# Folded attention weight in blocks of whole heads, moved to 128-row chunks by transfers within SBUF

## The chip, the core and the metric

One of the eight cores of a Trainium2 chip runs the kernel. A core has five engines, each with its own stream of instructions: TensorE (PE, matrix multiplication; PEld is its weight load), VectorE (DVE), ScalarE (ACT), GpSimd (POOL) and SyncE (SP), which here only issues transfers (DMA). The engines wait for one another through semaphores. The working memory SBUF has 128 partitions, and matmuls write to PSUM, eight banks of 512 float32 columns on 128 partitions. The metric is the device time of one execution in microseconds; the median of the runs is compared.

## The reference

The input x has 2048 tokens of 640 features in bfloat16. Both branches read the same layer-normalised x:

```python
xn = layernorm(x)
q, k, v = split(xn @ wqkv)                       # 32 heads of 20 features
pq, pk = phi(q), phi(k)                          # phi(t) = (t + 1 if t > 0 else exp(t)) + 1e-6
kv  = einsum("bhsd,bhse->bhde", pk, v)           # 20 x 20 for each head
z   = einsum("bhsd->bhd", pk)
num = einsum("bhqd,bhde->bhqe", pq, kv)
den = einsum("bhqd,bhd->bhq", pq, z)[..., None] + 1e-6
s   = merge_heads(num / den) @ wo                # 640 x 640
g   = silu(relu(xn @ w1) @ w2)                   # 640 -> 1728 -> 640
out = x + s * g
```

## The kernel before

All intermediate data stay in SBUF. Tokens are handled in 16 tiles of 128 or 4 chunks of 512, features in 5 chunks of 128 and the 1728 hidden features in 13 chunks of 128 and a rest of 64. The order of the work on each engine is the order in which the program text emits it; a small scheduler class only works out which semaphores an instruction has to wait for.

The program goes through these stages:

1. **Normalisation and projections** (to 111 us). x is loaded, normalised and transposed. Blocks of keys (`K_mm`, L473), queries (`Q_block`, L541) and hidden features (`H_mm`, L556) are interleaved on TensorE. ScalarE and VectorE form `pk`, `pqT` (transposed queries after phi) and `hT`. GpSimd adds up z. At the end stand `z_col` (L633; VectorE multiplies its result by a mask, L637), the last hidden blocks, the rest of 64 hidden features (`H_halves`, L578) and the denominators (`den`, L646), whose reciprocal VectorE takes (L654).
2. **Transfers behind it.** SP issues the loads of w2 (L756, L760), four stores that write the reciprocal denominators, each repeated for the 20 features of its head, to a scratch in HBM (L763), two loads of wo in blocks of 120 rows (L767, L769), and five loads that bring the scratch back as `rep` (L772). SP works its list in order.
3. **Gram blocks** (`G_block`, L787, 111 to 133 us). `GT = xn^T pk`, five blocks of 32 matmuls. ScalarE copies each block to SBUF (L792). Values are never formed: kv is `wv^T GT`, of which only the 20 x 20 blocks on the diagonal are kept.
4. **Folded weight** (133 to 153 us). `kv_block` (L799) multiplies, for six heads (120 rows) at a time, `wv^T GT`; VectorE masks the diagonal blocks into `kvp` (L802), a 640-column row of blocks whose other columns GpSimd has zeroed (L907). `W_block` (L813) then forms the product of kv and wo, `wf`, in five chunks of 128 rows. A chunk of 128 rows cuts through blocks of 120, so each chunk adds up two blocks, in two halves of 320 columns: 20 matmuls. The last block has only 40 rows. ScalarE copies each chunk to SBUF (L818). Between these stand pieces of the down projection `U_main` (L831), 13 matmuls of 320 columns for each tile and half, `U_halves` (L847) for the rest of 64, and the gate's silu (L862, L865). VectorE multiplies `pqT` by `rep` (`divide`, L778).
5. **Output tiles** (153 us to the end). `s_tile` (L877) is `pqT x wf`, 10 matmuls a tile; VectorE multiplies by the gate (L899) and adds x (L884), which has been loaded a second time (L909, issued after the gram blocks); SP stores the tile (L887). Each output tile stands between pieces of the down projection of the next pair of tiles.

The buffers share memory: `wo_sb` lies where x was loaded, `GT` and `wf` lie where the query and key weights were, `kvp` where `pk` was, `rep` and the gates where the transposed normalised x was, and the second x where the normalised x was. PSUM banks go round by hand: the gram blocks use banks 0 to 3, `kv_block` 0 to 3, the first pair of down-projection tiles 4 to 7.

The two loops that the change replaces are these:

```python
    U_main(0, 0)
    for c in range(VC):
        kv_block(c, c % 4)
    for m in range(C):
        divide(m)
    U_main(0, 1, (0,))
    W_block(0, 0)
    W_block(1, 2)
```

Of the kernel before, what the change touches and what calls it, by code (L numbers as in the profile page):

```python
# [211 lines left out]
def bass_recurrent_scan__linear_attn_block__dense_activation_relu__prompt_kernel(  # L212
# [26 lines left out]
    VR = HC * DH  # L239
    VC = -(-D // VR)  # L240

    def vrows(c):
        return min(VR, D - VR * c)

    def cs_of_m(m):
        return [c for c in range(VC) if VR * c < P * (m + 1) and VR * c + vrows(c) > P * m]

    x2 = A_x[0]
    out2 = out[0]
# [13 lines left out]
    NOUT = 4  # L263
    reg3 = nc.alloc_sbuf_tensor("reg3", [P, T * D], bf)
    pk = reg3[:, :].rearrange("p (t n) -> p t n", t=T)
    kvp = reg3[:, 0:VC * D].rearrange("p (c n) -> p c n", c=VC)
    outb = reg3[:, VC * D:(VC + NOUT) * D].rearrange("p (a n) -> p a n", a=NOUT)
    tmpo = reg3[:, (VC + NOUT) * D:(VC + 2 * NOUT) * D].rearrange("p (a n) -> p a n", a=NOUT)
    pqT = nc.alloc_sbuf_tensor("pqT", [P, C, S], bf)
# [12 lines left out]
    xq0 = wqk[:, :, D:D + 512]  # L282
    GT = reg6[:, 0:C * D].rearrange("p (c n) -> p c n", c=C)
    wf = reg6[:, C * D:2 * C * D].rearrange("p (c n) -> p c n", c=C)
    wv_sb = nc.alloc_sbuf_tensor("wv_sb", [P, C, D], bf)

    reg7 = nc.alloc_sbuf_tensor("reg7", [P, XR * D], bf)
# [35 lines left out]
    def dma(E, fn, R=(), W=(), extra=()):  # L323
        i = nds[0]
        nds[0] += 1
        return sc.dma(E, fn, i, R=R, W=W, extra=extra)
# [77 lines left out]
    def xnk(t, cs=range(C)):  # L404
        return [("xn", t, c) for c in cs]
# [300 lines left out]
    for j in range(1, J):  # L706
        qs = [("q", j, f) for f in range(C)]
        hs = [("h", j, f) for f in range(NF)]
        if j == J - 1:
            qs += [("q", 0, f) for f in range(C)]  # L710
        blocks = []
        while qs or hs:
            if qs:
                blocks.append(qs.pop(0))
            for _ in range(2 if j + 1 < J else 1):
                if hs:
                    blocks.append(hs.pop(0))
        for n, (kind, jj, f) in enumerate(blocks):
            if kind == "q":
                Q_block(jj, f)  # L720
            else:
                lastX = H_block(jj, f)
            if j + 1 < J:
                t0 = 4 * (j + 1)
                if n in (0, 2, 4, 6):
                    LN_stats(t0 + n // 2)
                if n in (1, 3, 5, 7):
                    LN_norm(t0 + n // 2)
                    xnT_dma(t0 + n // 2)
                if n in (9, 12, 14, 17):  # L730
                    t = t0 + (9, 12, 14, 17).index(n)
                    K_mm(t, 0)
                    K_ev(t, 0)
                if n in (8, 10, 12, 14, 16):
                    z_add()
                if j == 1 and n == 16:
                    build_masks()
            else:
                if n == 0:
                    for t in range(4):  # L740
                        dma("SP", lambda eng, t=t: eng.dma_start_transpose(xq0[:, :, tok(t)], xn[:, t, :]),
                            R=xnk(t), W=[("xq0", t)], extra=[lastK[0]])
                if n % 2 == 0 and zpend:
                    z_add()
                    if not zpend:
                        z_split()
                if n == 18:
                    z_col()
                if n == 20:
                    H_halves()  # L750
                    den()
    assert not zpend

    for a in range(2):
# [7 lines left out]
    for i in range(J):  # L762
        dma("SP", lambda eng, i=i: eng.dma_start(  # L763
            rscr[:, schunk(i)].rearrange("(h d) s -> h d s", d=DH),
            rden[H * i:H * (i + 1), :].unsqueeze(1).to_broadcast([H, DH, 512])), R=[("rden",)], W=[("rscr", i)])
    nfull = (VC - 1) * VR
    dma("SP", lambda eng: eng.dma_start(wo_sb[0:VR, 0:VC - 1, :], A_wo[0:nfull, :].rearrange("(c p) n -> p c n", p=VR)),  # L767
        W=[("wo", 0)], extra=[last_norm[0]])
    dma("SP", lambda eng: eng.dma_start(wo_sb[0:D - nfull, VC - 1, :], A_wo[nfull:D, :]),  # L769
        W=[("wo", 1)], extra=[last_norm[0]])  # L770
    for c in range(C):
        dma("SP", lambda eng, c=c: eng.dma_start(rep[:, c, :], rscr[P * c:P * (c + 1), :]),  # L772
            R=[("rscr", i) for i in range(J)], W=[("rep", c)], extra=[lastX])
# [20 lines left out]
        return ag  # L794

    def kv_block(c, b):
        n0, nr = VR * c, vrows(c)
        w = P if n0 + P <= D else nr
        sc.group("PE", [(lambda eng, k=k: eng.matmul(ps[b][0:w, 0:nr], lhsT=wv_sb[:, k, n0:n0 + w],  # L799
                                                     rhs=GT[:, k, n0:n0 + nr], start=(k == 0), stop=(k == C - 1)))  # L800
                        for k in range(C)], R=[("wv",)] + [("GT", k) for k in range(C)], W=[("ps", b)])
        sc.op("DVE", lambda eng: eng.tensor_tensor(  # L802
            out=kvp[0:nr, c, n0:n0 + nr].rearrange("p (h e) -> p h e", e=DH),
            in0=ps[b][0:nr, 0:nr].rearrange("p (h e) -> p h e", e=DH),
            in1=m6[0:nr, 0:nr // DH].unsqueeze(2).to_broadcast([nr, nr // DH, DH]), op=ALU.mult),
            R=[("ps", b), ("m6",), ("kvz",)], W=[("kv", c)])

    def W_block(m, b):
        cs = cs_of_m(m)
        fns = []  # L810
        for a in range(2):
            for ci, c in enumerate(cs):
                fns.append(lambda eng, a=a, c=c, ci=ci: eng.matmul(  # L813
                    ps[b + a][:, 0:HN], lhsT=kvp[0:vrows(c), c, P * m:P * (m + 1)],
                    rhs=wo_sb[0:vrows(c), c, HN * a:HN * (a + 1)],
                    start=(ci == 0), stop=(ci == len(cs) - 1)))
        sc.group("PE", fns, R=[("wo", 0), ("wo", 1), ("kvz",)] + [("kv", c) for c in cs], W=[("ps", b), ("ps", b + 1)])
        sc.op("ACT", lambda eng: eng.activation(out=two(wf[:, m, :]), in_=ps2(b, HN),  # L818
                                                func=ACTF.Copy), R=[("ps", b), ("ps", b + 1)], W=[("wf", m)])


    pairs = [(4 * jj + q, 4 * jj + q + 4) for jj in (0, 2) for q in range(4)]
# [46 lines left out]
    def s_tile(p, u, b, last=False):  # L869
        t = pairs[p][u]  # L870
        os_ = so[0] % NOUT
        so[0] += 1
        i = t // 4

        parts = [(b, 0, HN), (b + 1, HN, 512), (bank(7, 0), 512, D)] if last else [(b, 0, HN), (b + 1, HN, D)]
        for pb, lo, hi in parts:
            sc.group("PE", [(lambda eng, c=c, pb=pb, lo=lo, hi=hi: eng.matmul(  # L877
                ps[pb][:, 0:hi - lo], lhsT=pqT[:, c, tok(t)], rhs=wf[:, c, lo:hi],
                start=(c == 0), stop=(c == C - 1))) for c in range(C)],
                R=[("pqT", i, c) for c in range(C)] + [("wf", c) for c in range(C)], W=[("ps", pb)])  # L880
        gk = [("g", t, 0), ("g", t, 1)]

        def add(E, lo, hi, keys):
            sc.op(E, lambda eng: eng.tensor_tensor(out=outb[:, os_, lo:hi], in0=tmpo[:, os_, lo:hi],  # L884
                                                   in1=xre[:, t, lo:hi], op=ALU.add),
                  R=[("tmpo", os_, k) for k in keys] + [("xre", t // 4)], W=[("outb", os_, k) for k in keys])
            dma("SP", lambda eng: eng.dma_start(out2[tok(t), lo:hi], outb[:, os_, lo:hi]),  # L887
                R=[("outb", os_, k) for k in keys])

        if last:  # L890
            for k, (pb, lo, hi) in enumerate(parts):
                sc.op("DVE", lambda eng, pb=pb, lo=lo, hi=hi: eng.tensor_tensor(  # L892
                    out=tmpo[:, os_, lo:hi], in0=ps[pb][:, 0:hi - lo], in1=g_sb[:, t, lo:hi], op=ALU.mult),
                    R=[("ps", pb)] + gk, W=[("tmpo", os_, k)])
                if k == 0:
                    add("POOL", lo, hi, (0,))
            add("DVE", HN, D, (1, 2))
        else:
            sc.op("DVE", lambda eng: eng.tensor_tensor(  # L899
                out=two(tmpo[:, os_, :]), in0=ps2(b, HN), in1=two(g_sb[:, t, :]), op=ALU.mult),  # L900
                R=[("ps", b), ("ps", b + 1)] + gk, W=[("tmpo", os_, k) for k in range(3)])
            add("DVE", 0, D, (0, 1, 2))

    lastG = None
    for k in range(C):
        lastG = G_block(k, (0, 2)[k % 2])
    sc.op("POOL", lambda eng: eng.memset(kvp, 0.0), W=[("kvz",)], extra=[lastG])  # L907
    for jx in range(4):
        dma("SP", lambda eng, jx=jx: eng.dma_start(  # L909
            xre[:, 4 * jx:4 * jx + 4, :], x2[512 * jx:512 * (jx + 1), :].rearrange("(t p) n -> p t n", p=P)),  # L910
            W=[("xre", jx)], extra=[lastG])

    lo, hi = range(7), range(7, NF)
    U_main(0, 0)
    for c in range(VC):
        kv_block(c, c % 4)
    for m in range(C):
        divide(m)
    U_main(0, 1, (0,))
    W_block(0, 0)  # L920
    W_block(1, 2)
    U_main(0, 1, (1,))
    U_halves((0, 1))
    U_silu(0, 0)
    U_silu(0, 1)
    U_main(1, 0)
    W_block(2, 4)
    W_block(3, 6)
    U_silu(1, 0)
    U_main(1, 1, (0,))  # L930
    W_block(4, 4)
    U_main(1, 1, (1,))
    U_silu(1, 1)
    s_tile(0, 0, 4)
    s_tile(0, 1, 6)
# [53 lines left out]
```

## Time and profile before

| what | value |
|---|---|
| median of 3 runs | 224.97 us (224.68 to 225.07) |
| the profiled execution's own time | 224.7 us |
| its span | 223.0 us |
| granted TensorE clock | 1.0 throughout |
| TensorE busy | 97% of the span |
| VectorE, ScalarE, GpSimd busy | 51%, 38%, 21% |
| gram blocks, folded weight stage, output stage | 111.4 to 133.2, 133.2 to 152.9, 152.9 to 223.0 us |

The span runs from the first to the last instruction that the profile shows; the execution's own time has 1.7 us around it. Times in the rows count from the start of the span. In the rows of the timeline the columns are start, length (from the first start to the last end of a merged run of instructions), engine, line, operation, the tile written and those read, the shape, the count, and in brackets the idle time before it with what ended it. A matmul's own length (299 ns for 320 columns) is its passage through the array; the next one starts long before it has ended, so that the distance of two starts is what a matmul costs. `120*128` stands for a weight tile of 120 rows and 128 columns. In rows by line, the three numbers behind the count are the shortest, median and longest length in ns. In rows of waits the columns are the total, the number of times and the longest wait in us. In the rows of transfer issues the last number is the median time from issue to landing in us, and in the row of a stretch of time the last three are the granted clock, the transfer engines' busy share and GB/s. In rows of the chain the columns are start, length, engine, tile, line and count.

### The profile page before, as it was taken

What the parts mean: (1) busy time and instruction counts of PE and PEld (TensorE: products, weight loads), DVE (VectorE), ACT (ScalarE), POOL (GpSimd) and SP (SyncE); (2) the same over time, 40 slices, a digit from 0 to 9 for tenths busy, and PEclk for the clock granted to TensorE, in tenths of its full rate; (3) what the DMA queues carried; (4) which work ended last, traced back from release to release, by engine and by line L of the source; (5) the groups of instructions that cost most, each with busy time, mean ns of one, the idle gap of its engine ahead of it and who ended that gap; (6) DMA issues with size and microseconds to landing.
All of it is one profiled execution on the core that took longest, in us unless ns stands there. A gap on an engine that the chain in (4) does not pass through costs nothing.

```text
span 223.0 us, 3534 instructions
## 1 busy us (share of the span) xinstructions
PE 216.9 (97%) x1471; PEld 133.9 (60%) x1482; DVE 114.4 (51%) x193; ACT 85.3 (38%) x137; POOL 47.0 (21%) x67
## 2 busy tenths in 40 slices
PE   7999999999999999999999999999999999999993
PEld 2865554455545554444477777666767776776672
DVE  2788836789686999986330004803322222314062
ACT  2467765567656565555321120632021102110300
POOL 4053101269123998600000004000000000000001
PEclk9999999999999999999999999999999999999999
DMA  6899580211012105000089999940110100000011
GB/s 205 232 379 231 118 249 21 59 39 23 0 29 59 32 1 118 0 0 3 0 257 361 240 223 374 369 154 0 59 59 3 60 29 32 29 29 32 29 54 64
DMA packets 27432, 23.73 MB, mean 106 GB/s; under 512 B 11673, under 2 KB 26777, under 8 KB 27417
## 3 DMA queue, kind: packets, MB, share of 16 engines
q1 hardware_dynamic: 26761, 23.03, 35.1%
q10 hardware_dynamic: 656, 0.49, 0.7%
q8 instruction: 11, 0.18, 0.3%
q14 instruction: 4, 0.03, 0.0%
HBM read 15.65 MB, written 5.24 MB: 94 GB/s over the span
## 4 chain that ended last, share of the span: by engine, by line
PE 95%; DVE 1%; DMA 1%; issue 0%; ACT 0%
PE psT L831 26%; PE psT L556 25%; PE psT L787 10%; PE psT L473 10%; PE psT L541 10%; PE psT L877 9%; PE psT L813 1%; DMA reg<-in_A_x_dram 1%; PE psT L847 1%; PE psT L578 1%; PE psT L799 1%; PE psT L646 1%; PE psT L451 0%; DVE reg L892 0%; DVE stats L393 0%
## 5 line engine op out<-in xcount | busy, mean ns | idle before, releaser
L556 PE MATMUL psT<-reg 128*128 128x512 bf16 (+1 forms) x295 | 59.8, 347 | 0.7 <-issue 0.2
L831 PE MATMUL psT<-reg,hT 128*128 128x320 bf16 x416 | 60.2, 299 | 0.0
L831 PEld LDWEIGHTS psT<-reg,hT 128*128 128x128 bf16 x416 | 40.2, 98 | 16.6 <-issue 1.1
L556 PEld LDWEIGHTS psT<-reg 128*128 128x128 bf16 x305 | 27.3, 98 | 27.0 <-issue 0.4
L899 DVE TENSOR_TENSOR reg<-psT,reg 128x640 bf16<-128x640 f32 x15 | 12.4, 824 | 53.1 <-PE psT L877 53.1
L563 ACT ACTIVATE hT<-psT 128x512 bf16<-128x512 f32 x52 | 30.9, 599 | 19.4 <-PE psT L556 19.4
L865 ACT ACTIVATE reg<-psT 128x640 bf16<-128x640 f32 (+1 forms) x13 | 8.4, 661 | 42.8 <-PE psT L831 23.3
L541 PE MATMUL psT<-reg 128*128 128x512 bf16 x99 | 24.6, 379 | 0.1
L473 PE MATMUL psT<-reg 128*128 128x320 bf16 x160 | 24.2, 299 | 0.0
L482 POOL TENSOR_TENSOR zacc<-zacc,reg 128x640 f32<-128x640 f32 x16 | 23.7, 1483 | 1.9 <-DVE reg L516 1.0
L877 PE MATMUL psT<-reg,pqT 128*128 128x320 bf16 (+2 forms) x165 | 24.0, 295 | 0.0
L787 PE MATMUL psT<-reg 128*128 128x320 bf16 x160 | 21.9, 299 | 0.0
L473 PEld LDWEIGHTS psT<-reg 128*128 128x128 bf16 x160 | 15.6, 98 | 8.2
L877 PEld LDWEIGHTS psT<-reg,pqT 128*128 128x128 bf16 x165 | 15.9, 98 | 6.0
L787 PEld LDWEIGHTS psT<-reg 128*128 128x128 bf16 x160 | 15.6, 98 | 6.2
L884 POOL TENSOR_TENSOR reg<-reg 128x320 bf16<-128x320 bf16 x1 | 0.8, 786 | 82.6 <-DVE reg L892 82.6
L551 DVE SCALAR_TENSOR_TENSOR pqT<-er 128x512 bf16<-128x512 bf16 x20 | 17.1, 854 | 0.7
L541 PEld LDWEIGHTS psT<-reg 128*128 128x128 bf16 x100 | 9.7, 98 | 11.6 <-DVE er L549 0.6
L393 DVE BATCH_NORM_STATS2 stats<-reg 128x6 f32<-128x320 bf16 x32 | 14.0, 479 | 3.4 <-DMA reg<-in_A_x_dram 3.4
L548 ACT ACTIVATE er<-psT 128x512 bf16<-128x512 f32 x20 | 12.0, 598 | 8.9 <-PE psT L541 8.1
L549 DVE TENSOR_SCALAR er<-psT 128x512 bf16<-128x512 f32 x20 | 13.6, 679 | 3.0 <-ACT er L548 3.0
L516 DVE TENSOR_TENSOR reg<-ek 128x640 bf16<-128x640 bf16 x16 | 13.5, 843 | 1.5 <-ACT ek L507 1.0
(67 smaller groups left out, 137.7 us busy)
## 6 DMA issues: line engine op xcount, KB each, us to landing
reg<-in_A_x_dram SPq DMA_DIRECT2D x16, 160.0 KB, 3.8
rscr<-rden SPq DMA_DIRECT2D x4, 640.0 KB, 10.8
reg<-rscr SPq DMA_DIRECT2D x5, 512.0 KB, 8.5
reg<-in_A_x_dram SPq DMA_DIRECT2D x4, 640.0 KB, 11.5
out_dram<-reg SPq DMA_DIRECT2D x15, 160.0 KB, 1.8
reg<-in_A_wqkv_dram SPq DMA_DIRECT2D x2, 800.0 KB, 6.7
reg<-in_B_w_dram SPq DMA_DIRECT2D x1, 1120.0 KB, 5.6
reg<-in_B_w_dram SPq DMA_DIRECT2D x1, 1040.0 KB, 7.7
```

The lines of the kernel that those rows point to most:

```text
L393: sc.op("DVE", lambda eng, a=a: eng.bn_stats(stats[:, t, a, :], xv[:, HN * a:HN * (a + 1)]), R=[("xin", t % XR)], W=[("stats", t, a)])
L473: fns.append(lambda eng, a=a, k=k: eng.matmul(ps[b + a][:, 0:HN], lhsT=xnT[:, k, tok(t)], rhs=wqk[:, k, D + HN * a:D + HN * (a + 1)], star ...
L482: sc.op("POOL", lambda eng: eng.tensor_tensor(out=zacc[:, :], in0=zacc[:, :], in1=pk[:, t, :], op=ALU.add), R=[("zacc",), ("pk", t)], W=[( ...
L516: sc.op("DVE", lambda eng: eng.tensor_tensor(out=pk[:, t, :], in0=e_, in1=r_, op=ALU.add), R=[("ek_e", es), ("ek_r", es)], W=[("pk", t)])
L541: sc.group("PE", [(lambda eng, k=k: eng.matmul(ps[b], lhsT=wqk[:, k, P * f:P * (f + 1)], rhs=rhs(k), start=(k == 0), stop=(k == C - 1))) f ...
L549: sc.op("DVE", lambda eng: eng.tensor_scalar(out=r_, in0=ps[b], scalar1=0.0, scalar2=1e-6, op0=ALU.max, op1=ALU.add), R=[("ps", b), ("er_e ...
L551: sc.op("DVE", lambda eng: eng.scalar_tensor_tensor(out=pqT[:, f, schunk(j)], in0=e_, scalar=1.0, in1=r_, op0=ALU.min, op1=ALU.add), R=[(" ...
L556: return sc.group("PE", [(lambda eng, k=k: eng.matmul(ps[b][:, lo:hi], lhsT=w1_sb[:, k, P * f:P * (f + 1)], rhs=xnT[:, k, 512 * j + lo:512 ...
L563: sc.op("ACT", lambda eng: eng.activation(out=hT[:, f, schunk(j)], in_=ps[b], func=ACTF.Relu), R=[("ps", b)], W=[("hT", j, f)])
L787: fns.append(lambda eng, t=t, a=a: eng.matmul(ps[b + a][:, 0:HN], lhsT=xn[:, t, P * k:P * (k + 1)], rhs=pk[:, t, HN * a:HN * (a + 1)], sta ...
L831: sc.group("PE", [(lambda eng, f=f, n=n: eng.matmul(ps[b + n][:, 0:HN], lhsT=hT[:, f, tok(t)], rhs=w2_sb[:, f, HN * n:HN * (n + 1)], start ...
L877: sc.group("PE", [(lambda eng, c=c, pb=pb, lo=lo, hi=hi: eng.matmul(ps[pb][:, 0:hi - lo], lhsT=pqT[:, c, tok(t)], rhs=wf[:, c, lo:hi], sta ...
```

## The change

The folded weight is now formed in the blocks of 120 rows themselves, each by two matmuls, since a block of six whole heads needs no other block. The sixth block starts at row 520 in place of 600, so that it too has 120 rows; of these only the last 40 are used. The zeros around the blocks, and the memset that writes them, go. ScalarE copies block 0 to its place in `wf`; the other five go to a staging buffer that lies where `GT` was, and SP moves their rows into the 128-row chunks of `wf` by transfers within SBUF: two each for blocks 1 to 4 (8 + 112, 16 + 104, 24 + 96, 32 + 88 rows) and one for block 5 (40 rows). The output tiles wait for all of these.

The weights that `kv_block` loads are now 120 columns wide in all six blocks; before, five of them were 128 wide with 120 used, and the last 40.

The order changes too. The six `kv_block`s stand behind 7 matmuls of the down projection, where they stood behind 26, and the folded blocks are spread over the first pair's down projection. The second load of x is issued behind the last move instead of right after the gram blocks. The loads of wo stand behind the four transposes of the first chunk (L741) on SP instead of between the stores and loads of the denominators. `den` stands ahead of `H_halves`.

```diff
+    V0 = [min(VR * c, D - VR) for c in range(VC)]
...
-    kvp = reg3[:, 0:VC * D].rearrange("p (c n) -> p c n", c=VC)
+    kvp = reg3[:, 0:VC * VR].rearrange("p (c n) -> p c n", c=VC)
...
+    wh = GT
...
                     for t in range(4):
                         dma("SP", lambda eng, t=t: eng.dma_start_transpose(xq0[:, :, tok(t)], xn[:, t, :]),
                             R=xnk(t), W=[("xq0", t)], extra=[lastK[0]])
+                    dma("SP", lambda eng: eng.dma_start(
+                        wo_sb[0:VR, 0:VC - 1, :], A_wo[0:VR * (VC - 1), :].rearrange("(c p) n -> p c n", p=VR)),
+                        W=[("wo", 0)], extra=[last_norm[0]])
+                    dma("SP", lambda eng: eng.dma_start(wo_sb[0:VR, VC - 1, :], A_wo[D - VR:D, :]),
+                        W=[("wo", 1)], extra=[last_norm[0]])
...
                 if n == 20:
+                    den()
                     H_halves()
-                    den()
...
-    nfull = (VC - 1) * VR
-    dma("SP", lambda eng: eng.dma_start(wo_sb[0:VR, 0:VC - 1, :], A_wo[0:nfull, :].rearrange("(c p) n -> p c n", p=VR)),
-        W=[("wo", 0)], extra=[last_norm[0]])
-    dma("SP", lambda eng: eng.dma_start(wo_sb[0:D - nfull, VC - 1, :], A_wo[nfull:D, :]),
-        W=[("wo", 1)], extra=[last_norm[0]])
...
     def kv_block(c, b):
-        n0, nr = VR * c, vrows(c)
-        w = P if n0 + P <= D else nr
-        sc.group("PE", [(lambda eng, k=k: eng.matmul(ps[b][0:w, 0:nr], lhsT=wv_sb[:, k, n0:n0 + w],
-                                                     rhs=GT[:, k, n0:n0 + nr], start=(k == 0), stop=(k == C - 1)))
+        n0 = V0[c]
+        sc.group("PE", [(lambda eng, k=k: eng.matmul(ps[b][0:VR, 0:VR], lhsT=wv_sb[:, k, n0:n0 + VR],
+                                                     rhs=GT[:, k, n0:n0 + VR], start=(k == 0), stop=(k == C - 1)))
                         for k in range(C)], R=[("wv",)] + [("GT", k) for k in range(C)], W=[("ps", b)])
...
+    def W_block(c, b):
+        sc.group("PE", [(lambda eng, a=a: eng.matmul(
+            ps[b + a][0:VR, 0:HN], lhsT=kvp[0:VR, c, :], rhs=wo_sb[0:VR, c, HN * a:HN * (a + 1)],
+            start=True, stop=True)) for a in range(2)], R=[("wo", 0), ("wo", 1), ("kv", c)],
+            W=[("ps", b), ("ps", b + 1)])
+        if c == 0:
+            dst, keys = wf[0:VR, 0, :], [("wf", 0, 0)]
+        else:
+            dst, keys = wh[0:VR, c - 1, :], [("GT", c - 1)]
+        sc.op("ACT", lambda eng: eng.activation(out=two(dst), in_=ps2(b, HN)[0:VR], func=ACTF.Copy),
+              R=[("ps", b), ("ps", b + 1)], W=keys)
+        if c > 0:
+            lo, hi = VR * c, V0[c] + VR
+            for m in (lo // P, (hi - 1) // P):
+                r0, r1 = max(lo, P * m), min(hi, P * (m + 1))
+                if ("wf", m, c) in wfk:
+                    continue
+                wfk.append(("wf", m, c))
+                dma("SP", lambda eng, m=m, r0=r0, r1=r1: eng.dma_start(
+                    wf[r0 - P * m:r1 - P * m, m, :], wh[r0 - V0[c]:r1 - V0[c], c - 1, :]),
+                    R=keys, W=[("wf", m, c)])
...
-    sc.op("POOL", lambda eng: eng.memset(kvp, 0.0), W=[("kvz",)], extra=[lastG])
...
-    U_main(0, 0)
+    U_main(0, 0, (0,), range(7))
     for c in range(VC):
         kv_block(c, c % 4)
     for m in range(C):
         divide(m)
+    W_block(0, 6)
+    U_main(0, 0, (0,), range(7, NF))
+    W_block(1, 0)
+    W_block(2, 2)
+    U_main(0, 0, (1,))
+    W_block(3, 0)
+    W_block(4, 2)
     U_main(0, 1, (0,))
-    W_block(0, 0)
-    W_block(1, 2)
+    W_block(5, 0)
+    x_again()
     U_main(0, 1, (1,))
...
     U_main(1, 0)
-    W_block(2, 4)
-    W_block(3, 6)
     U_silu(1, 0)
-    U_main(1, 1, (0,))
-    W_block(4, 4)
-    U_main(1, 1, (1,))
+    U_main(1, 1)
```

More of the change, by code (lines that the diff above doesn't have):

```diff
@@ L240, in bass_recurrent_scan__linear_attn_block__dense_activation_relu__prompt_kernel @@
     VC = -(-D // VR)
[L242 to L246, printed above, removed]
+    V0 = [min(VR * c, D - VR) for c in range(VC)]
     x2 = A_x[0]
@@ L801, in kv_block @@
                         for k in range(C)], R=[("wv",)] + [("GT", k) for k in range(C)], W=[("ps", b)])
         sc.op("DVE", lambda eng: eng.tensor_tensor(
[L803 to L819, printed above, removed]
@@ new lines, in kv_block @@
+            out=kvp[0:VR, c, :].rearrange("p (h e) -> p h e", e=DH),
+            in0=ps[b][0:VR, 0:VR].rearrange("p (h e) -> p h e", e=DH),
+            in1=m6[0:VR, 0:HC].unsqueeze(2).to_broadcast([VR, HC, DH]), op=ALU.mult),
+            R=[("ps", b), ("m6",)], W=[("kv", c)], extra=[lastG])
+    def W_block(c, b):
[19 more added lines that the diff above has]
+                    R=keys, W=[("wf", m, c)])
@@ L822, in bass_recurrent_scan__linear_attn_block__dense_activation_relu__prompt_kernel @@
+    wfk = [("wf", 0, 0)]
     pairs = [(4 * jj + q, 4 * jj + q + 4) for jj in (0, 2) for q in range(4)]
@@ L879, in s_tile @@
                 start=(c == 0), stop=(c == C - 1))) for c in range(C)],
-                R=[("pqT", i, c) for c in range(C)] + [("wf", c) for c in range(C)], W=[("ps", pb)])
+                R=[("pqT", i, c) for c in range(C)] + wfk, W=[("ps", pb)])
         gk = [("g", t, 0), ("g", t, 1)]
@@ L906, in bass_recurrent_scan__linear_attn_block__dense_activation_relu__prompt_kernel, with x_again @@
         lastG = G_block(k, (0, 2)[k % 2])
[L907 to L913, printed above, removed]
-    U_main(0, 0)
+    def x_again():
+        for jx in range(4):
+            dma("SP", lambda eng, jx=jx: eng.dma_start(
+                xre[:, 4 * jx:4 * jx + 4, :], x2[512 * jx:512 * (jx + 1), :].rearrange("(t p) n -> p t n", p=P)),
+                W=[("xre", jx)], extra=[lastG])
+    U_main(0, 0, (0,), range(7))
     for c in range(VC):
```

## The prediction

> **What bounds the kernel now.** I read the page first (busy shares, granted clock, chain), then TensorE's waits, then the order of time around the folded weight, then the queue of transfers.
>
> ```profile
> PE 216.9 (97%) x1471; PEld 133.9 (60%) x1482; DVE 114.4 (51%) x193; ACT 85.3 (38%) x137; POOL 47.0 (21%) x67
> PEclk9999999999999999999999999999999999999999
> DMA  6899580211012105000089999940110100000011
> PE 95%; DVE 1%; DMA 1%; issue 0%; ACT 0%
> ```
>
> TensorE (PE) is busy for 97% of the span at full clock in every slice, and 95% of the chain that ended last runs over it. The longest of its waits is in the start-up, before anything that the change touches:
>
> ```profile
> PE psT L355 <- PEq L974: 0.8, 1, 0.8
> ```
>
> So the end is set by the stream of matmuls alone, and a change is worth what it takes out of that stream or what hole it makes in it. A busy PE is not a PE at its peak, so I price the stream by distances between starts:
>
> ```profile
> 133.01 3.69 PE L831 MATMUL psT<-reg,hT 128*128 128x320 bf16 x26
> 133.22 0.70 ACT L792 ACTIVATE reg<-psT 128x640 bf16<-128x640 f32 x1 [3.64 <-PE psT L787]
> 133.24 3.30 POOL L907 MEMSET reg<- 128x3840 bf16 x1 [40.13 <-PE psT L787]
> 136.55 1.70 PE L799 MATMUL psT<-reg,wv_sb 128*128 128x120 bf16 x30
> 138.18 1.94 PE L831 MATMUL psT<-reg,hT 128*128 128x320 bf16 x13
> 138.40 5.75 DVE L778 TENSOR_TENSOR pqT<-pqT,reg 128x2048 bf16<-128x2048 bf16 x5
> 139.96 1.25 PE L813 MATMUL psT<-reg 120*128 120x320 bf16 x8
> 141.05 1.93 PE L831 MATMUL psT<-reg,hT 128*128 128x320 bf16 x13
> 147.10 1.25 PE L813 MATMUL psT<-reg 120*128 120x320 bf16 x8
> 148.19 1.93 PE L831 MATMUL psT<-reg,hT 128*128 128x320 bf16 x13
> 149.96 1.02 PE L813 MATMUL psT<-reg 120*128 120x320 bf16 x4
> 150.91 1.94 PE L831 MATMUL psT<-reg,hT 128*128 128x320 bf16 x13
> 152.69 2.88 PE L877 MATMUL psT<-reg,pqT 128*128 128x320 bf16 x20
> ```
>
> A matmul of 320 columns takes (136.55 - 133.01) / 26 = 0.136 us. The folded weight (L813) takes 141.05 - 139.96 = 1.09 for its first eight, 1.09 for the next eight, and 150.91 - 149.96 = 0.95 for the last four, which at 0.136 would be 0.54. Two of these four contract over 40 rows only, and their shape on the array differs:
>
> ```profile
> L813 PEld LDWEIGHTS psT<-reg x20: 93/98/99, 139.8 to 150.7; 120*128 120x128 bf16 x18, 40*128 40x128 bf16 x2
> ```
>
> The excess of 0.41 is four changes of shape, 0.10 each. The eighteen of 120 rows show none: eight in 1.09 is the plain 0.136.
>
> **The change, part by part.**
>
> *Folded weight.* Twenty matmuls become twelve, all 120 rows deep: 12 x 0.136 = 1.63 against 1.09 + 1.09 + 0.95 = 3.13. That is -1.50 us, on the path.
>
> *Value-side products (L799 before).* Thirty stay. The first 25 have this row:
>
> ```profile
> 136.55 1.48 PE L799 MATMUL psT<-reg,wv_sb 128*128 128x120 bf16 x25
> 137.95 0.19 PEld L799 LDWEIGHTS psT<-reg,wv_sb 128*40 128x40 bf16 x5
> L799 PEld LDWEIGHTS psT<-reg,wv_sb x30: 96/98/99, 136.4 to 138.0; 128*128 128x128 bf16 x25, 128*40 128x40 bf16 x5
> L799 PE MATMUL psT<-reg,wv_sb x30: 178/216/217, 136.5 to 138.1; 128*128 128x120 bf16 x25, 128*40 128x40 bf16 x5
> ```
>
> With 216 ns for the last one, the distance is (1.48 - 0.216) / 24 = 53 ns. All six blocks now have 120 columns: 30 x 0.053 = 1.58, against 138.18 - 136.55 = 1.63, which held two changes of shape for the 40-column block. That is -0.05. But the weights loaded are now 120 columns wide, where they were 128. No row has that load. The narrow ones bound it: five loads of 40 columns span 0.19, so they follow each other by (0.19 - 0.097) / 4 = 23 ns; and for 64 columns (L578) two loads span 0.11 and four span 0.14:
>
> ```profile
> 105.64 0.11 PEld L578 LDWEIGHTS psT<-reg 128*64 128x64 bf16 x2 [0.42 <-ACT hT L563]
> 105.64 0.14 PEld L578 LDWEIGHTS psT<-reg 128*64 128x64 bf16 x4 [0.42 <-ACT hT L563]
> ```
>
> The second pair, into the same columns, follows 0.03 us behind the first, under 0.47 ns a column, so 120 columns need about 0.05 to 0.056. That is the length of the matmul they hide beside, so I take 54 ns, 1.62 in all: -0.01. The ends are 53 ns (-0.05) and the whole 98 ns that any load shows (2.94, so +1.31). In the twelve folded-weight matmuls the load hides behind 0.136.
>
> The row says that the load of 128 columns keeps up with 53 ns. [...]
>
> *Split of the down projection.* 7 matmuls instead of 26 now stand between the last gram block and the value products. They cover 133.01 + 7 x 0.136 = 133.96; the copy of the last gram block ends at 133.22 + 0.70 = 133.92, and the memset of 3.30 us, for which 26 were needed, is gone. I take +0.03 for the semaphore; ends 0 and 0.15 (the load can't run ahead by its 0.13). The other pieces keep their number, 52 + 52.
>
> *Where each folded block waits.*
>
> ```profile
> L802 DVE TENSOR_TENSOR reg<-psT,m x6: 192/282/283, 137.0 to 138.3; 120x120 bf16<-120x120 f32 x5, 40x40 bf16<-40x40 f32 x1
> 92.51 1.08 PE psT L556 x5
> 93.59 1.08 PE psT L541 x5
> ```
>
> Block 1 stands six matmuls behind block 0 and needs the sixth masking on VectorE; maskings follow the products by one, 0.28 each, so it is ready about 0.5 us ahead. Blocks 3, 4 and 5 reuse banks emptied by ScalarE (0.70 a copy) 13 matmuls (1.77 us) earlier. Two copies take 1.40. Cost 0; without the 13 matmuls it would be up to 0.8 each. The first output tile now waits for nine landings, where it waited for two engines. Waits that are already met show no gap: the L541 group at 93.59, the first to read the four transposes of chunk 0, starts where the one before it ends (92.51 + 1.08). Cost 0.
>
> *Denominators ahead of the half chunks.*
>
> ```profile
> 105.30 0.32 DVE L637 TENSOR_TENSOR zmat<-mh,psT 128x160 bf16<-128x160 f32 x1
> 107.92 1.26 PE L646 MATMUL psT<-pqT,zmat 128*32 128x512 bf16 x20
> 109.96 3.35 DVE L654 RECIPROCAL rden<-denS 128x512 bf16<-128x512 f32 x1
> 113.81 7.51 SPq L763 DMA_DIRECT2D rscr<-rden  x4
> ```
>
> The mask product ends at 105.62; the denominators would start at 105.64. I take +0.03 (ends 0 and 0.1; the number of shape changes is the same). The reciprocal ends 2.3 us earlier, at about 111.0 instead of 113.31, but the stores issue at 113.81 behind the w2 loads on SP, so nothing comes of it.
>
> *Queue of transfers.*
>
> ```profile
> 82.76 5.16 SPq L741 DMA_TRANSPOSE reg<-reg  x4
> 121.36 3.23 SPq L767 DMA_DIRECT2D reg<-in_A_wo_dram  x1
> 130.22 2.27 SPq L772 DMA_DIRECT2D reg<-rscr  x5
> 133.21 7.22 SPq L909 DMA_DIRECT2D reg<-in_A_x_dram  x4
> reg<-reg SPq DMA_TRANSPOSE x16, 2.6
> reg<-in_A_x_dram SPq DMA_DIRECT2D x4, 640.0 KB, 11.5
> 155.11 0.49 DVE L884 TENSOR_TENSOR reg<-reg 128x640 bf16<-128x640 bf16 x1
> 144.00:146.00 2.00, 2.00 (x17) 1.45 (x15) 0.15 (x1) 1.06 (x2) 0.00 (x0) 1.00 1.07 362
> ```
>
> The wo loads (two issues) go behind the four transposes, to about 88 us, where the DMA row of the page reads 0 (slices of 5.6 us); nothing stands behind them there until w2 at 111 us, and wo is there long before its new first use at 135.6. The replicated reciprocals (L772) still issue at 130.2, when the stores have landed, but no longer behind wo. The divisions start at about 136.3 and end after 5.75 us, 142; they are first needed at about 144 (gate) and 151.2 (output tiles). That leaves the last ones over 7 us, and they do not land later than now, when the divisions ran without a gap from 138.40. The nine moves (five blocks, 520 rows of 1.25 KB) wait on SP for ScalarE's copies; behind each stand only later moves, the x loads and the stores of the output. By the sum the last block's matmuls end at 141.6 and its copy at 142.4. Moves lie nearest to the SBUF transposes, 2.6 us, so the last lands at about 145.5, and the first output tile asks at 151.2. The cover is 5.7 us: cost 0. Behind the last move stand the four x loads (142.8 instead of 133.2). 2.6 MB at 362 GB/s take 7.2 us, so all are in by about 152, the first at 147; the first addition (155.11 now) asks at about 153.7. At the 11.5 us of now it would be 0.6 late, on VectorE alone: TensorE needs a bank that is emptied behind that addition only at the second tile of the next pair, some 5 us on (a pair's first tile, 26 + 10 matmuls at 0.136).
>
> *Sum.* -1.50 - 0.01 + 0.03 + 0.03 = -1.45 us. From the last folded block on the stream is the same. The profiled execution took 224.70 (span 223.0 and 1.7 around it), so 223.25; the median of the runs shown, 224.97, stands 0.27 above it: 223.5 on that scale. 0.2% (0.45 us) is about what a measurement here can tell from no change.
>
> **The rivals.**
>
> *A load of 120 columns paces the products.* If each of the thirty takes the 98 ns of a whole load, 2.94 - 1.62 = +1.32, leaving -0.13: 224.9, no change. For it: no row has such a load, and 53 ns is already no more than it needs. Against: 40 and 64 columns come at under 0.6 ns a column. [...]
>
> *120 columns count as another shape.* Eight changes (in and out at four places) at 0.10: +0.8, 224.3. Against: 120 rows don't.
>
> *The other side: the load does not overlap at all.* If the array streams nothing while 120 columns load, each of 42 loads (30 and 12) costs about 0.052: +2.2, so +0.75, 225.7. It decides from 1.45 / 42 = 35 ns a load on. Against: loads of 64 columns run beside matmuls of 512 (twenty in 107.92 - 105.64 = 2.28, two at a time).
>
> *The moves come late.* If the last takes 11.5 us to land, as x does now, it is there at 153.9, the first output tile waits 2.7 us, and the sum is +1.25: 226.2. It decides from 8.8 us of landing on. Against: the moves stand ahead of x, and the queue before them is empty.
>
> **How the numbers follow.** My forecast 0.70, alone 223.1 to 223.9. Shape 0.09 (faster). Paced by loads 0.09 (same). No overlap 0.07 and late moves 0.05 (slower). Faster is 0.79, same 0.09, slower 0.12. The range, 223.1 to 224.9, starts at the gain with 53 ns and no waits (-1.55, 223.4), less the 0.3 by which the fastest run shown (224.68) lies below the median, reaches to the paced case and leaves out 0.12.
>
> **What would show it.** Right: twelve 120 x 320 matmuls 0.136 apart; thirty products 53 to 56 ns apart; the first output tile at about 151.2; no wait of TensorE on a DMA. Wrong: products at 98 ns, idle weight loads of 0.1 at each change between L799, L808 and L841 of the new kernel, or a first output tile that waits for a move.

## The result

The changed kernel takes 222.93 us (median of 6 runs, 222.82 to 223.15) against 224.96 for the kernel before (6 runs, 224.68 to 225.07). The ratio is 0.9914, with a 95% interval of 0.9901 to 0.9927: between 1.6 and 2.2 us faster. Forecast were 223.5 and a range that began at 223.1. The direction was right, and the time fell just below the range.

Its profile, the lines that answer to those of before. First the page: the span, the busy shares, the granted clock, the transfer row and the chain by engine.

```profile
span 221.4 us, 3528 instructions
PE 215.8 (97%) x1463; PEld 133.9 (60%) x1474; DVE 114.6 (52%) x193; ACT 86.1 (39%) x138; POOL 43.7 (20%) x66
PEclk9999999999999999999999999999999999999999
DMA  6899581211012105800059969369110101000002
PE 95%; DVE 1%; DMA 1%; issue 0%; ACT 0%
```

TensorE is still the bound. The transfers moved: wo is now loaded around 92 us, and the block that was full from 112 to 147 us has holes. The order of time in the folded-weight stage of the changed kernel:

```profile
133.34 1.11 PE L841 MATMUL psT<-reg,hT 128*128 128x320 bf16 x7
133.54 0.70 ACT L791 ACTIVATE reg<-psT 128x640 bf16<-128x640 f32 x1 [3.64 <-PE psT L786]
134.30 1.86 PE L797 MATMUL psT<-reg,wv_sb 128*120 128x120 bf16 x30
136.00 0.44 PE L808 MATMUL psT<-reg 120*120 120x320 bf16 x2
136.27 0.98 PE L841 MATMUL psT<-reg,hT 128*128 128x320 bf16 x6
136.40 5.76 DVE L777 TENSOR_TENSOR pqT<-pqT,reg 128x2048 bf16<-128x2048 bf16 x5
137.09 0.71 PE L808 MATMUL psT<-reg 120*120 120x320 bf16 x4
137.63 1.93 PE L841 MATMUL psT<-reg,hT 128*128 128x320 bf16 x13
138.29 7.04 SPq L825 DMA_DIRECT2D reg<-reg  x9
139.40 0.71 PE L808 MATMUL psT<-reg 120*120 120x320 bf16 x4
139.94 1.93 PE L841 MATMUL psT<-reg,hT 128*128 128x320 bf16 x13
141.71 0.44 PE L808 MATMUL psT<-reg 120*120 120x320 bf16 x2
141.99 1.93 PE L841 MATMUL psT<-reg,hT 128*128 128x320 bf16 x13
145.38 2.50 SPq L919 DMA_DIRECT2D reg<-in_A_x_dram  x4
151.57 2.88 PE L887 MATMUL psT<-reg,pqT 128*128 128x320 bf16 x20
```

From the first down-projection matmul to the first output tile the stage took 152.69 - 133.01 = 19.68 us before and takes 151.57 - 133.34 = 18.23 now; with the starts to the nanosecond it is 19.67 and 18.23, so -1.44. The twelve folded-weight matmuls take 0.27 + 0.54 + 0.54 + 0.28 = 1.63.

The output tiles gave nothing. The last addition on VectorE, which ends the chain, stands here before and after:

```profile
219.61 0.52 DVE L884 TENSOR_TENSOR reg<-reg 128x320 bf16<-128x320 bf16 x1
```

```profile
218.49 0.52 DVE L894 TENSOR_TENSOR reg<-reg 128x320 bf16<-128x320 bf16 x1
```

From the first output tile to the end of this addition both take 67.44 us. But from there to the end of the span it is 222.96 - 220.13 = 2.83 us before and 221.43 - 219.02 = 2.41 now. That is a second gain, of 0.42 us, at a place where I had expected none. The table gives six profiled executions by these stretches (the last four rows are from the experiments below; the starts of matmuls and the spans are to 0.01 us from the trace). The column "idle" is from the trace's records of SyncE, which the views leave out: it is the time between the end of its last wait for a landing and the start of its last branch. "Last fetch" is the start of the last transfer of 8192 bytes on the instruction queue (q14) on which, in an experiment below, 128 more instructions of SyncE bring one transfer more.

```
us                       first    gram    gram to   first tile  last add  idle   last    span
                         gram     blocks  1st tile  to last add to end           fetch
before                   111.28   21.73   19.67     67.44       2.83      0.47   223.20  222.96
changed                  111.61   21.73   18.23     67.44       2.41      0.05   196.20  221.43
before, again            111.76   21.73   19.67     67.45       2.84      0.47   223.68  223.45
before, 4 more on SP     111.40   21.73   19.67     67.45       2.42      0.05   219.05  222.68
before, 128 more on SP   111.51   21.73   19.67     67.44       2.73      0.37   223.33  223.09
changed, 119 more on SP  111.75   21.73   18.23     67.44       2.72      0.37   222.40  221.87
```

The start of the first gram block differs between executions of the same kernel by 0.5 us (111.28 and 111.76): the start-up scatters, nearly all of it in the first 7 us (the same copy on VectorE starts at 6.02 and at 6.51). The two profiled executions compared first, 222.96 and 221.43 us of span, stand only 1.53 apart, because the changed one started 0.33 later.

### The profile page after: what moved, and what is told of

It is laid out like the page before. It is cut to its first block, busy times and chain, and to the rows that moved or that the text cites. A ratio compares the mean times of both kernels' runs of the same rounds, so it can differ in the third digit from the quotient of the medians.

```text
span 221.4 us, 3528 instructions
## 1 busy us (share of the span) xinstructions
PE 215.8 (97%) x1463; PEld 133.9 (60%) x1474; DVE 114.6 (52%) x193; ACT 86.1 (39%) x138; POOL 43.7 (20%) x66
## 4 chain that ended last, share of the span: by engine, by line
PE 95%; DVE 1%; DMA 1%; issue 0%; ACT 0%
PE psT L841 26%; PE psT L555 25%; PE psT L472 10%; PE psT L786 10%; PE psT L540 10%; PE psT L887 10%; DMA reg<-in_A_x_dram 1%; PE psT L857 1%; PE psT L577 1%; PE psT L797 1%; PE psT L808 1%; PE psT L645 1%; PE psT L450 1%; DVE reg L902 0%; DVE stats L392 0%
```

## Experiments

**The kernel before, once more.** No edit.

> The kernel before, unchanged, profiled a second time. In the profiles compared so far the changed kernel gained 1.44 us between the last gram block and the first output tile, nothing in the output tiles, and 0.43 us between the last addition on VectorE (end at 220.13 before, 219.01 after) and the end of the span (222.96 and 221.43). Theory A (the end of SyncE's instruction list costs 0.42 us in this build, each time): SyncE's last branch starts about 0.47 us after the last landing is seen, and 2.8 us lie between the last addition and the end, as in the first profile. Theory B (the ends scatter from one execution to the next): the 2.8 us differ, anywhere from 2.4 to 2.8. Time: the same as before, ratio 1.000 within 0.001.

225.07 us, ratio 1.0011 (0.9989 to 1.0033). The end took 2.84 us, with the same idle 0.47 us ahead of SyncE's last branch. The end doesn't scatter: it belongs to the build. Theory A holds so far. In the eight profiled executions that the table leaves out the end is 2.83 us where SyncE's list is as long as in the kernel before, and 2.40 to 2.42 where it has four or nine instructions more.

**Four more instructions on SyncE.**

```diff
+    sc.ops["SP"].append(("wait", [("E", "PE", 1 + i % 8) for i in range(8)], None, None))
     for a in range(2):
         c0, c1 = (0, 7) if a == 0 else (7, NF)
```

> The kernel before with eight waits, four instructions on SyncE, that are long met, put ahead of the loads of w2 where SyncE stands idle. Nothing else moves. Theory A (a boundary in SyncE's instruction list falls on the last branch and costs 0.42 us there; four instructions more move it ahead of the waits for the last landings, where it is hidden): 2.4 us between the last addition and the end, time about 224.5 (-0.42 us, ratio 0.998). Theory B (scatter, or something that the moves and the order changed): 2.8 us and 224.95, ratio 1.000.

224.41 us, ratio 0.9981 (0.9973 to 0.9990). The end takes 2.42 us, the idle time is 0.05, and every stage is as before. The last addition and the span in its profile:

```profile
219.73 0.53 DVE L885 TENSOR_TENSOR reg<-reg 128x320 bf16<-128x320 bf16 x1
```

```profile
span 222.7 us, 3549 instructions
```

Four instructions that do nothing make the kernel before 0.4 us faster. The length of SyncE's list matters, with nothing else of the change in place.

**128 more instructions on SyncE.** The same line with `range(256)`. It tries a period of 128 instructions, an assumption of the author's that no run before it had shown.

> The same with 256 met waits, 128 instructions on SyncE. [...] Theory A with that period: the boundary is back on the last branch, 2.8 us between the last addition and the end, and 224.95. [...] Theory B: whatever the first profile showed, 2.8 us.

224.95 us, ratio 1.0012 (0.9995 to 1.0030). The end takes 2.73 us and the idle time is 0.37: 0.31 of the 0.42 is back, as a period of 128 instructions would have it; with another period it could have stayed at the 2.42 us of the run with four. The trace shows one more fetch of 8192 bytes, at 91.8 us where the added waits run, and the last one again at 223.3, behind the end. With four more instructions the last one comes at 219.05, while SyncE has yet to wait for the last stores; in the changed kernel at 196.2.

**The boundary put back into the changed kernel.** The same line in the changed kernel with `range(238)`: its SyncE list is nine transfers longer than before, and 128 - 9 = 119.

> The changed kernel with 238 met waits, 119 instructions on SyncE, ahead of the loads of w2. Its SyncE list is 9 instructions longer than that of the kernel before, so with a period of 128 instructions 119 more put the boundary where the kernel before had it. Theory A: the last branch starts 0.37 to 0.47 us after the wait before it, 2.75 to 2.85 us lie between the last addition and the end instead of 2.41, and the time rises to 223.3 (ratio 0.993). If the boundary is not what the end of the kernel before paid for: 222.95, ratio 0.991.

223.37 us, ratio 0.9930 (0.9918 to 0.9943). The end takes 2.72 us, just under the 2.75 to 2.85 that were expected, the idle time is 0.37, and the stage is 18.23 as it should be. The last addition and the span:

```profile
218.63 0.52 DVE L895 TENSOR_TENSOR reg<-reg 128x320 bf16<-128x320 bf16 x1
```

```profile
span 221.9 us, 3647 instructions
```

So 0.3 to 0.4 us of the change's gain come from the nine transfers' making SyncE's list longer, whatever they transfer.

**The narrow contraction of 40 rows alone.** In the kernel before:

```diff
-                    ps[b + a][:, 0:HN], lhsT=kvp[0:vrows(c), c, P * m:P * (m + 1)],
-                    rhs=wo_sb[0:vrows(c), c, HN * a:HN * (a + 1)],
+                    ps[b + a][:, 0:HN], lhsT=kvp[0:VR, c, P * m:P * (m + 1)],
+                    rhs=wo_sb[0:VR, c, HN * a:HN * (a + 1)],
```

> The kernel before, in which the two folded-weight matmuls that contract over the last block's 40 rows contract over 120 (the other 80 rows of the zeroed buffer add nothing to the result). The number of matmuls stays at twenty. By the prediction, four changes of shape at 0.10 us go: the last four folded-weight matmuls take 0.54 us instead of 0.95, and the time falls by 0.41 us, to 224.55 (ratio 0.998). If the shape is not what costs there, 0.95 us and 224.95.

```profile
151.89 0.71 PE L813 MATMUL psT<-reg 120*128 120x320 bf16 x4
152.43 1.93 PE L831 MATMUL psT<-reg,hT 128*128 128x320 bf16 x13
```

The four take 152.43 - 151.89 = 0.54, and the stage 19.26 instead of 19.67: -0.41, as worked out. In the kernel before, each of the four distances between starts at a change of rows, into 40 and out of them, is 0.23 to 0.24 us in the trace (149.96, 150.19, 150.43, 150.67, 150.91), so each change costs 0.10, the matmul of 120 rows ahead of it included. The median is 224.41, but the ratio of 0.9989 (0.9974 to 1.0004) decides nothing, since one of the ten runs, the profiled one of 226.21 us, started 1.5 to 1.9 us late. The stage shows it; the times alone don't.

**Both small parts on the kernel before.** The last two edits together, with the eight waits.

> The kernel before with its last folded-weight matmuls 120 rows deep (0.41 us less in the profile alone) and four more instructions on SyncE (0.42 us less at the end). Both lie on the path and in different places, so they add up: 224.95 - 0.83 = 224.1, ratio 0.996, with 19.26 us between the last gram block and the first output tile and 2.41 us at the end. If one of them was only scatter of the start: 224.5.

224.10 us, ratio 0.9959 (0.9945 to 0.9973); 19.25 us and 2.42 us. They add up. Of the change's gain, 0.83 us could be had with no restructuring at all; the rest of the stage, 18.23 against 19.25, is eight matmuls fewer (8 x 0.136 = 1.09) less the 0.07 that the value-side products lost.

**Loads of 128 columns again.** In the changed kernel:

```diff
+        w = P if n0 + P <= D else VR
-        ... ps[b][0:VR, 0:VR], lhsT=wv_sb[:, k, n0:n0 + VR],
+        ... ps[b][0:w, 0:VR], lhsT=wv_sb[:, k, n0:n0 + w],
```

> The changed kernel with weight loads of 128 columns again in the first five of the six value-side products (25 of the 30 loads), as before the change; the sixth keeps 120. Measured in the changed kernel: 55 ns from one product to the next with loads of 120 columns, and the loads take 0.135 us instead of 0.098. Theory A (a load of 120 columns takes about as long as the product beside it): 53 ns for the first 25, 1.62 us in all instead of 1.70, time 222.85 (ratio to the kernel before 0.991). Theory of the paced products (each load serial or near 98 ns): would need 98 ns in the changed kernel, and is out already; nothing more than 0.1 us can come back here.

The products in this kernel (first and second row) and, below them, the two rows of the changed kernel that give the loads by their shortest, median and longest length:

```profile
134.27 1.76 PE L798 MATMUL psT<-reg,wv_sb 128*128 128x120 bf16 x30
135.87 0.44 PE L809 MATMUL psT<-reg 120*120 120x320 bf16 x2
```

```profile
L797 PEld LDWEIGHTS psT<-reg,wv_sb x30: 129/135/135, 134.3 to 135.9; 128*120 128x120 bf16 x30
L797 PE MATMUL psT<-reg,wv_sb x30: 218/218/263, 134.3 to 135.9; 128*120 128x120 bf16 x30
```

135.87 - 134.27 = 1.60 us against 136.00 - 134.30 = 1.70: loads of 120 columns cost 0.10 us in all. Each takes 135 ns, where loads of 128 take 98, but a load runs beside the product ahead of it, and the distance grows only from 53 to 55 ns; the first one has nothing to hide behind, so that 100 ns lie between the first two products, and it gives the rest. The median of 223.02 (ratio 0.9924, 0.9899 to 0.9949) can't show 0.1.

**x issued ahead of the moves.** In the changed kernel `x_again()` right after the gram blocks.

> The changed kernel with the second load of x issued right after the gram blocks again, ahead of the moves. Theory A (the moves have 5 to 6 us of cover, and only where they stand behind x is it used up): the x issues hold SyncE, in the kernel before until 140.4, so the moves issue later and land behind 2.6 MB of x, at about 148 to 150; the first output tile at 151.6 does not wait, and the time is 222.9, ratio 0.991. Rival (x ahead of the moves makes the first output tile wait): a wait of TensorE on a move, up to 3 us, and 223 to 226.

223.03 us, ratio 0.9915 (0.9899 to 0.9932), stage 18.23, no wait of TensorE on a transfer. The place of the second x load gains no time here, but it decides how much of the cover is left. The moves in the changed kernel, and below them in this one:

```profile
L825 SPq DMA_DIRECT2D reg<-reg x9: 552/767/969, 138.3 to 144.6; - x9
DMA to landing us min/median/max: 1.9/2.1/2.7
```

```profile
L825 SPq DMA_DIRECT2D reg<-reg x9: 551/776/947, 138.1 to 144.5; - x9
DMA to landing us min/median/max: 7.1/8.4/10.1
```

The views count only part of the nine landings. By all nine in the trace, a move behind x lands 4.9 to 10.1 us after its issue, in place of 1.9 to 2.7. The last of them is there at 150.1 in this kernel, 1.2 us ahead of the first output tile (151.4), and at 146.8 in the changed kernel, 4.8 us ahead of it (151.6).

**wo at its old place.** In the changed kernel the two loads stand ahead of the loads of the reciprocals again.

> The changed kernel with the loads of wo back between the stores and the loads of the reciprocal denominators on SyncE. The first folded-weight matmuls now ask for wo at 136.0, where they asked at 140.0 before the change. In the kernel before, wo landed 14.4 us after its issue at 121.4, so at 135.8, and its second part a little later. Theory A (the move of wo was needed for the new order, though not by much): the first folded block waits 0 to 1 us, and the divisions start later than 136.4, at about 138; 222.9 to 224. If wo lands at 138 or later, 225.

```profile
L765 SPq DMA_DIRECT2D reg<-in_A_wo_dram x1: 2135/2135/2135, 122.2 to 122.2; - x1
DMA to landing us min/median/max: 13.1/13.1/13.1
L768 SPq DMA_DIRECT2D reg<-in_A_wo_dram x1: 2137/2137/2137, 124.4 to 124.4; - x1
DMA to landing us min/median/max: 11.5/11.5/11.5
136.11 0.44 PE L808 MATMUL psT<-reg 120*120 120x320 bf16 x2
```

The two parts land at 122.2 + 13.1 = 135.3 and 124.4 + 11.5 = 135.9, and the first folded-weight matmul starts at 136.1. The stage is 18.23: no wait, by 0.2 us. The divisions start at 137.1, a little ahead of the 138 expected. Of the profiled execution's 223.26 us nothing is due to wo. The median of 223.69 (ratio 0.9954, 0.9927 to 0.9982) lies higher than the stretches explain; some runs of this series reach 225.8, and what those lost isn't in this profile; with only 0.2 us to spare, a wait for wo in them can't be ruled out. In the profiled execution the early load is a cover, not a gain.

**Three matmuls of cover instead of seven.** In the changed kernel:

```diff
-    U_main(0, 0, (0,), range(7))
+    U_main(0, 0, (0,), range(3))
...
-    U_main(0, 0, (0,), range(7, NF))
+    U_main(0, 0, (0,), range(3, NF))
```

> The changed kernel with 3 instead of 7 down-projection matmuls between the last gram block and the value-side products; the other four follow later, so that the work is the same. The copy of the last gram block ends 0.70 us after the matmuls that it waits for; 3 matmuls cover 0.41 us, 7 cover 0.95. By the prediction TensorE waits about 0.5 us at the first product (0.54 less the 0.04 that seven leave): the time rises from 222.93 to 223.4 (ratio 0.993). If something else than this copy is what the products wait for, no change.

Waits of TensorE and its loads in this kernel (total, times, longest; the second row counts from the last load, the first from the last matmul):

```profile
PE psT L797 <- ACT reg L791: 0.4, 1, 0.4
PEld psT L797 <- ACT reg L791: 0.7, 1, 0.7
```

The stage takes 18.77, +0.54 against an expected 0.50. The median of 223.76 us (ratio 0.9953, 0.9937 to 0.9969) lies above the 223.4 that was expected; the stretches don't show the rest. Seven are just enough: the first product of the changed kernel starts at 134.30, 0.96 us behind the seven's first start, where 7 x 0.136 is 0.95.

**The last block's move late.** The variant with x early, with the last folded block 13 matmuls ahead of the first output tile.

```diff
-    W_block(5, 0)
     U_main(0, 1, (1,))
...
-    U_main(1, 1)
+    U_main(1, 1, (0,))
+    W_block(5, 4)
+    U_main(1, 1, (1,))
```

> The changed kernel with x issued early, as in the run that showed no cost of that, and the last folded block (one move of 40 rows) put 13 down-projection matmuls ahead of the first output tile, the place where the kernel before had its last chunk. Theory A (a move costs its copy, issue and landing, about 0.2 + 0.70 + 0.1 + 2.1 us behind the matmuls, and is free only under more cover than that): 13 matmuls cover 1.77, so TensorE waits about 1.3 to 1.6 us at the first output tile for a landing, and the time is 224.4 (222.95 + 1.45), within 0.3. Rival (moves within SBUF are hidden in any place): 222.95.

```profile
149.52 0.44 PE L808 MATMUL psT<-reg 120*120 120x320 bf16 x2
149.80 1.93 PE L841 MATMUL psT<-reg,hT 128*128 128x320 bf16 x13
150.00 0.70 ACT L816 ACTIVATE reg<-psT 120x640 bf16<-120x640 f32 x1 [1.25 <-PE psT L808]
150.73 0.76 SPq L825 DMA_DIRECT2D reg<-reg  x1
153.06 2.56 PEld L887 LDWEIGHTS psT<-reg,pqT 128*128 128x128 bf16 x20 [1.66 <-DMA reg<-reg]
153.06 2.89 PE L887 MATMUL psT<-reg,pqT 128*128 128x320 bf16 x20 [1.33 <-DMA reg<-reg]
```

TensorE stands idle for 1.33 us at the first output tile and the stage takes 19.72, 1.49 more. From the start of the matmuls that follow the folded block, 149.80, to the tile are 3.26 us: 0.20 to the copy, 0.70 for it, 0.03 to the issue, 2.33 from there to the use. The profiled execution took 224.65, inside what was expected; the median of 224.93 (ratio 1.0020, 0.9989 to 1.0052) lies 0.3 above that. This one block in the old place would have eaten the stage's whole gain (19.72 against 19.67 before the change); the end of the program kept its own, at 2.40 us.

**Best of the parts.** The changed kernel with loads of 128 columns and the denominators behind the half chunks.

> The changed kernel with loads of 128 columns in five of the six products (0.10 us less between the last gram block and the first output tile when tried alone) and the denominators behind the half chunks again (the stretch from the last key block to the first gram block is 28.89 us in the changed kernel and 28.85 before it, so 0.04 less). 222.93 - 0.14 = 222.8, ratio 0.990; too small a gain over the changed kernel for the times to show, so the stretches in the profile decide: 18.13 and 28.85 us.

222.85 us, ratio 0.9907 (0.9894 to 0.9921); 18.13 us in the stage, and 28.86 us from the last key block to the first gram block (28.85 before, 28.89 changed). It is the fastest measured, by 0.1 us in the stretches; the times can't tell it from the changed kernel.

## Why the prediction was wrong, step by step

The sum on TensorE's path was right to 0.05 us (-1.45 forecast, -1.44 and +0.04 measured), its single terms to 0.08. What failed is the step "*Sum*": "From the last folded block on the stream is the same. The profiled execution took 224.70 (span 223.0 and 1.7 around it), so 223.25". It took the stream's end for the kernel's end and carried the 2.83 us behind the last addition over unchanged. They are 2.41 in the changed kernel, and -0.42 is missing from the sum. The range held 0.3 us for scatter at its lower end and nothing for this. That the profiled execution of the changed kernel took 223.15 us, close to the 223.25 of the sum, is luck: it started 0.33 us later than the one before, which hides most of the 0.42.

| step | predicted | measured |
|---|---|---|
| folded weight, 20 to 12 matmuls and no change of shape | -1.50 | -1.50 |
| value-side products | -0.01 | +0.07 (1.63 to 1.70) |
| cover by seven matmuls | +0.03 | +0.01 |
| denominators first | +0.03 | +0.04 (28.85 to 28.89) |
| output tiles | 0 | 0 (67.44 both) |
| end, behind the last addition | 0 | -0.42 |
| sum | -1.45 | -1.80 |

The stretches give -1.44 in the stage, +0.04 ahead of it and -0.42 at the end, -1.82 in all; the table's -1.80 is the same within the rounding of its terms. The medians stand 2.03 apart, and the interval, 1.6 to 2.2, holds -1.82. From 224.97 the stretches alone lead to 223.15, just inside the range; it took the last 0.2 too to fall below it. That 0.2 is probably scatter of the start-up, which differs by 0.5 us between executions, but no run isolates it. It didn't come back in the variant with x early, whose stretches are the same: its median is 1.85 below that of the kernel before in its series. The kernel of the last experiment has such a rest: 2.19, where its stretches give 1.95.

Point by point:

- *What bounds the kernel.* Right as far as it goes: 97% and 95% are unchanged, and every edit that touched the stream moved its stage in the profile by what was worked out, to 0.04 us. But "the end is set by the stream of matmuls alone" left 2.83 us behind the chain unread. The chain ends with an instruction, not with the program.
- *Four changes of shape at 0.10.* Right: 0.41 alone, and 0.10 at each of the four.
- *Loads of 120 columns.* Taken were 54 ns between 53 and 98, from loads of 40 and 64 columns; it is 55. The first one, exposed, adds 0.05 (100 ns from the first product to the second). The 98 ns were not "the whole 98 ns that any load shows": the loads of 64 columns took 110 in the kernel before (L578), those of 128 take 98, and these take 135, but the length does not set the distance: at 135 ns each, the products follow each other at 55. All three rivals that rest on these loads fall. The change of shape from 128 to 120 columns cost nothing here: folded blocks and down projections follow each other at 0.136 without a hole.
- *Cover of seven.* Right: 0.01 lost, and 0.54 with three.
- *Moves.* Right that they are hidden. SyncE took 0.55 to 0.97 us for each of the nine, so that the last was issued at 144.6 and x at 145.4, not 142.4 and 142.8; the cover was 4.8 us and not 5.7. The rival that has them late came near with x ahead of them, where 1.2 us of cover were left, and is real where the cover is gone: 1.33 us of waiting.
- *Queue of transfers.* Right that neither wo nor x is on the path: the profiled executions with one of them put back kept the stage at 18.23. The four parts of x landed at 149.6 to 156.5 us, later than the 147 to 152 that were worked out, and neither TensorE nor VectorE waited for them.
- *Denominators.* Right: +0.04, and nothing gained.
- *The length of SyncE's list.* It was read for what its waits delay, and nine transfers more were priced at the cover of their landings. That they also shift every later instruction of that list was not considered.

## What to carry to other kernels

Read what lies between the end of the chain and the end of the span, and compare it first when a change adds or removes instructions on the engine that closes the program; here 0.3 to 0.4 us came and went with the length of its list, and belong to no idea that the change embodies. On a kernel bound by TensorE, distances between starts priced each term of this change in that engine's stream to 0.08 us, also for loads that no row showed but narrower ones bounded. And a transfer in place of matmuls pays only under its full latency of other work: copy, issue and landing, 3.3 us here, and with a landing of 5 to 10 us in place of 2 to 3 where 2.6 MB of x stood ahead of it.

## What the runs showed that was not expected

SyncE's last branch started 0.47 us after its last wait in the kernel before (twice), 0.05 with four more instructions, and 0.37 with 128 more; in the changed kernel 0.05, and 0.37 with 119 more. A period of 128 instructions fits all six; 64 or 32 would fit as well, since 4, 9 and 128 are the only shifts that were tried. The trace has four fetches on the instruction queue (q14) within the span of the kernel before and five in the changed kernel, each of 8192 bytes, and 128 more instructions brought one more. That a boundary between two such fetches falls on the branch is how I read it; no run shows it. What the branch then waits for isn't shown: the last fetch stands 0.2 to 0.5 us behind the end of the span in these kernels, so it isn't that one. Why the idle time is 0.37 in two builds and 0.47 in the other stays open too.
